# A list scheduler's table of durations and its random term, changed together in a transformer-block kernel

## The chip, the cores and the metric

One core of one Trainium2 chip. The metric is the device time of one execution in microseconds (us); lower is better. The kernel before was run three times: 789.57 us (median), 788.88 and 794.04.

## The reference

One transformer block with adaptive layer norm, on 2048 rows of 512 columns, 32 heads of width 16, in bf16:

```python
mod = (silu(c) @ w_mod).reshape(1, 6, 1, 512)            # sa, ca, ga, sb, cb, gb
h = layernorm(x) * (1 + ca) + sa
q, k, v = split(h @ wqkv)                                # 32 heads, Dh = 16
p = softmax(q @ k.T * Dh ** -0.5)                        # 2048 x 2048 for each head
x = x + ga * ((p @ v).reshape(2048, 512) @ wo)
h = layernorm(x) * (1 + cb) + sb
out = x + gb * (gelu(h @ w1 + b1) @ w2 + b2)             # hidden width 1376
```

The bulk of the work is the exponentials of 32 x 2048 x 2048 scores.

## The kernel before, in words

**Tiling.** Queries go in 4 blocks of 512, keys in 16 tiles of 128. A *run* is four heads over one query block (in the last block: eight heads over half of it); there are 32 runs. For each run and key tile the four heads' scores are made by four matmuls that use 32 rows of the array each. One such piece, 128 keys x 512 queries of one head, is a *unit*: 32 x 16 x 4 = 2048 units in all.

**Two ways to an exponential.** A unit takes one of two ways.

- *ScalarE's way* (`qk_a`, L834): two or three units at a time are put into a PSUM tile `st` (one of three banks, one of two), and one ACTIVATE of 128x1536 or 128x1024 (L872) writes the exponentials to `pt`. One pass of matmuls with V follows for each key tile (`pv_op`, L934, matmuls at L961, into the accumulator `od`).
- *VectorE's way* (`qk_d`, L885, and `shifts`, L923): each unit of a key tile goes to a PSUM tile `ax`; an operation on VectorE (L913) turns it into the bit pattern of a coarse exponential, `ph`. Then four operations of 128x2048 (L928) make shifted copies `sh`; all five patterns are multiplied with copies of V that are scaled to fit (`VX`), so that their errors cancel. A key tile thus costs eight operations on VectorE and five passes of matmuls with V in place of one.

Only key tiles 2, 6, 10 and 14 of a run (in the first run only 14) may go VectorE's way. `next_tile` (L802) decides while the schedule is made: ScalarE first takes a run's other tiles, and then takes a shared tile too if VectorE has not taken it by then.

**Around it.** Layer norm, projections and transposes of the next blocks (`layer_norm`, `make_k`, `make_q`, `make_v`), and for each finished query block the output projection, second layer norm and feed-forward part (`block_tail`, L1154; for the last half block `last_half`, L1224) are strewn between the scores. Each block's Gelu (L1203) makes ScalarE change its function table before and after.

**The order.** The kernel writes out the order of every engine by itself. `Plan` (L103) is a list scheduler that runs while the program is built: each `Op` names its engine, its duration in us, its latency, what it depends on and which buffer it takes. `Plan.step` commits, again and again, the operation with the earliest possible start over all engines. On one engine, `pick` (L146) looks at all that could start within a short slack of the first, and takes the lowest `dyn + spread`: `dyn` (L350) is the priority, for TensorE by the state of the plan (scores for ScalarE 0.0, 2.2 or 6.0; scores for VectorE 1.0; matmuls with V 0.2 or 3.0), and `spread` (L158) is a pseudo-random addition. The planned clock `now` exists only while building; the chip gets four fixed instruction lists and the semaphores. The durations thus do not set how long anything takes. They set which order is written, and how many key tiles go each way.

When the plan finds TensorE idle for too long, it inserts matmuls of zeros (`heat`, L428; `zeros`, L446) that change no result.

The durations in question: `A_US` (L297) is an ACTIVATE of exponentials by its units; `0.6` at L915, L930, L986 and others is an operation of VectorE on 512 float32 columns of PSUM (or 2048 int16 columns of SBUF).

Of the kernel before, what the change touches and what calls it, by code (L numbers as in the profile page):

```python
# [12 lines left out]
ALU = mybir.AluOpType  # L13
# [44 lines left out]
DL = 0.14  # L58
DPL = 0.08
AL = 0.21  # L60
FILL = 1.6
SPREAD = 0.15
SEEDS = (917, 884, 957, 158, 587, 98, 234, 513, 13, 197, 564, 221, 161, 230, 162, 26, 317, 634, 72, 409, 524, 986, 200, 52, 57, 427, 804, 124, 15, 75, 621, 299)
HEAT = 1.3


# [39 lines left out]
class Plan:  # L106
# [49 lines left out]
        return s, o  # L156

    def spread(self, o):  # L158
        x = ((sum(map(ord, o.kind)) if o.eng == "PE" else o.fn.__code__.co_firstlineno if o.fn else 0) * 2654435761 ^ SEEDS[min(int(self.now // 25.0), len(SEEDS) - 1)] * 2246822519) & 0xFFFFFFFF
        x = ((x ^ x >> 15) * 2246822519) & 0xFFFFFFFF  # L160
        return SPREAD * ((x ^ x >> 13) & 1023) / 1024.0

    def ahead(self, can):

# [94 lines left out]
def kernel(  # L259
# [14 lines left out]
    nc = tc.nc  # L274
# [19 lines left out]
    MM = 0.2155  # L294
    SPAN = (3, 2)
    POOL_US, POOL_MIN = 0.68, 0.5
    A_US = {1: 0.475, 2: 0.904, 3: 1.33}  # L297
    AHEAD = 3
    PSUM_F = 8
    FIRST_DKS, D_TIME = (14,), 8.0  # L300
# [335 lines left out]
    def layer_norm(src, deps, mod, mod_dep, hold_z, alloc_h, engines, ps_res, kind, prio,  # L636
                   after=None, nt=TPB):

        ln = op("NIL", None, 0.0, (), lat=0.0, prio=0.0, acq=r_ln)
        st = [op("DVE", lambda o, t=t: stats(ln, t, src(t)), 0.83, (deps[t], ln, after and after[t]), prio=prio)  # L640
              for t in range(nt)]
        rs = [op("POOL", lambda o, i=i: rstd(ln, 2 * i, 2 * i + 2), 1.3,
                 st[2 * i:2 * i + 2] + [o_mh], prio=0.0) for i in range(nt // 2)]
        z = op("NIL", None, 0.0, (rs[0], hold_z), lat=0.0, prio=0.0, acq=r_z)
        za = [op("DVE", lambda o, t=t: apply(ln, z, t, src(t)), 0.33, (z, rs[t // 2]), prio=prio,
                 rel=(ln,), port=True) for t in range(nt)]
        h = op("NIL", None, 0.0, (rs[0],), lat=0.0, prio=0.0, acq=alloc_h)
        done = []
        trs = []
        if isinstance(ps_res, tuple):  # L650
            two = []
            for part in range(2):
                for half in range(2):
                    def tr(o, half=half, part=part):
                        if part:
                            o.tile = two[half].tile
                            two[half].ps = o.tile.bitcast(BF16)
                        ps = o.tile.bitcast(BF16)
                        for j in (2 * half, 2 * half + 1):
                            for t in (2 * part, 2 * part + 1):  # L660
                                nc.tensor.transpose(
                                    out=ps[:, (j % 2) * QB + t * P:(j % 2) * QB + (t + 1) * P],
                                    in_=z.tile[:, t, j * P:(j + 1) * P], identity=ident)
                    one = op("PE", tr, 4 * 0.0705, za[0:2 + 2 * part] + [o_id] + two[half:half + part],
                             lat=PEL, mode=("full", 0), kind=kind,
                             acq=None if part else ps_res[half], rel=(z,))
                    two.append(one)
            trs += two[2:4]
            for half in range(2):
                one, done_tr = two[half], two[2 + half]  # L670
                for j in (2 * half, 2 * half + 1):
                    e = engines[j]
                    done.append(op(e, lambda o, j=j, e=e, one=one: modulate(
                        e, h.tile[:, j, :], one.ps[:, (j % 2) * QB:(j % 2 + 1) * QB], mod, j),
                        0.5 if e == "DVE" else 0.72, (done_tr, mod_dep, h), prio=0.2, rel=(one,)))
        else:
            for j in range(NC):
                def tr(o, j=j):
                    o.ps = o.tile.bitcast(BF16)[:, 0:nt * P]
                    for t in range(nt):  # L680
                        nc.tensor.transpose(out=o.ps[:, t * P:(t + 1) * P],
                                            in_=z.tile[:, t, j * P:(j + 1) * P], identity=ident)
                one = op("PE", tr, nt * 0.0705, za, lat=PEL, mode=("full", 0), kind=kind,
                         acq=r_ax, rel=(z,))
                trs.append(one)
                e = engines[j]
                done.append(op(e, lambda o, j=j, one=one, e=e: modulate(
                    e, h.tile[:, j, 0:nt * P], one.ps, mod, j), 0.13 + nt * 0.1, (one, mod_dep, h), prio=0.1,
                    rel=(one,)))
        return h, done, za, trs  # L690
# [16 lines left out]

    def make_k(b, cc, kind, acq, eng, after=None):
        mm = proj(b, o_w[1], cc, kind, acq, after)
        o_k[(cc, b)] = op(eng, lambda o: copy(eng, kT[cc][b], mm.tile[:, 0:QB]), 0.6 if eng == 'DVE' else 0.5, (mm,), prio=0.3,  # L710
                          rel=(mm,))

    o_qz = [op("POOL", lambda o, n=n, p=p: nc.gpsimd.memset(QM[n][:, p, :], 0.0), 0.5, prio=0.5 + n)
# [2 lines left out]
    def make_q(b, cc, kind, acq):  # L716
        qm = op("NIL", None, 0.0, (), lat=0.0, prio=0.0, acq=r_qm)
        mm = proj(b, o_w[0], cc, kind, acq, after=qm)
        if (b, cc) == (0, 0):
            evs = [op("DVE", lambda o, p=p: nc.vector.tensor_scalar(  # L720
                out=qm.tile[:, p, :], in0=mm.tile[:, 0:QB], scalar1=qmask[:, p:p + 1], scalar2=None,
                op0=ALU.mult), 0.6, (mm, qm, o_mask), prio=0.1 if p == 0 else 0.45, rel=(mm,)) for p in range(2)]
        else:
            qs = op("DVE", lambda o: nc.vector.tensor_scalar(
                out=o.tile, in0=mm.tile[:, 0:QB], scalar1=QSC, scalar2=None, op0=ALU.mult), 0.6, (mm, qm),
                prio=0.3, acq=r_qs, rel=(mm,))

            evs = []
            for p in range(2):
                rows = [dma(lambda o, at=slice(i, i + 16), p=p: nc.sync.dma_start(  # L730
                    out=qm.tile[at, p, :], in_=qs.tile[at, :]), [qs] + o_qz, kb=16, n=1.4, prio=0.4 + p, rel=(qs,))
                    for i in range(16 * p, P, 32)]
                evs.append(op("NIL", None, 0.0, rows, lat=0.0, prio=0.0))
        o_q[(cc, b)] = (qm, evs)
        qm.uses += 1
        q_left[(cc, b)] = 8 * NT

    def make_v(b, cc, kind, acq, eng, after=None):
# [9 lines left out]
        def ev(o):  # L748
            dst = VEB[b][:, :, 8 * cc * VW:8 * (cc + 1) * VW].rearrange(
                "p t (h w) -> p t h w", w=VW)  # L750
            copy(eng, dst[:, :, :, 0:16], mm.tile[:, 0:QB].rearrange("p (t h d) -> p t h d", t=TPB, h=8))
        got = [op(eng, ev, 0.6, [mm] + o_v0[b], prio=0.3, rel=(mm,))]
        for t in DKS:
            if t // TPB == b:
                def scale(o, t=t):
# [129 lines left out]
    def qk_d():  # L885
# [24 lines left out]
        def ex(e):  # L910
# [1 line left out]
            units[0] += 1  # L912
            nc.vector.tensor_scalar(out=ph.tile[:, o.row * QB:(o.row + 1) * QB], in0=o.tile, scalar1=PH_B,  # L913
                                    scalar2=0.0, op0=ALU.add, op1=ALU.max)
        d_e.append(op("DVE", ex, 0.6, (o,), lat=DL, prio=0.5, rel=(o,)))  # L915
        d_e[-1].run = r
        if last:
            shifts(r, kt, ph, list(d_e))
# [4 lines left out]
    def shifts(r, kt, first, es):  # L923
        def parts(o):
            return lambda: [o.tile[:, h * QB:(h + 1) * QB].bitcast(BF16) for h in range(4)]
        pv_op(r, kt, 0, es, parts(first), (first,))
        for j in range(1, NPH):
            sh = op("DVE", lambda o, j=j: nc.vector.tensor_scalar(  # L928
                out=o.tile, in0=first.tile, scalar1=PH_SH[j], scalar2=None, op0=ALU.add),
                0.6, es, lat=DL, prio=2.0, acq=r_sh, rel=(first,), port=True)  # L930
            sh.run = r
            pv_op(r, kt, j, (sh,), parts(sh), (sh,))

# [49 lines left out]

    def normalise(r):
        last, od = o_last[r], o_od[r]
        OD = op("DVE", lambda o: nc.vector.tensor_copy(out=o.tile, in_=od.tile), 0.6, (last,),  # L986
                prio=0.0, acq=r_OD, rel=(od,))
        st = {}

# [164 lines left out]
    def block_tail(b, nt=TPB):  # L1154
# [8 lines left out]
        for t in range(nt):  # L1163
# [1 line left out]
                      [x for u in ots for x in u.two] + [prev], kind, r_ax, ots, 2)  # L1165
            prev = a
            res_done.append(op("DVE", lambda o, t=t, a=a: nc.vector.tensor_tensor(
                out=x2.tile[:, t, :], in0=a.tile, in1=xr.tile[:, t, :], op=ALU.add), 0.6,
                (a, xr), prio=0.1, rel=(a,)))
        h, hd, za, trs = layer_norm(lambda t: x2.tile[:, t, :], res_done, modB, o_late["mB"],  # L1170
                                    None, r_blk, ("DVE",) * 4, r_ax, kind, 0.3, None, nt)
# [10 lines left out]
        for f in range(NF):  # L1182
# [6 lines left out]
            if direct:  # L1189
# [3 lines left out]
                continue  # L1193
            ev.append(op("DVE", lambda o, f=f, mm=mm: nc.vector.tensor_scalar(  # L1194
                out=g.tile[:, f, 0:N], in0=mm.tile[:, 0:N], scalar1=b1c[:, f:f + 1], scalar2=None,
                op0=ALU.add), 0.13 + nt * 0.134, (mm, o_late["b1"]), prio=0.3 if part else 0.1, rel=(mm,)))
        if part:
            ge = [op("ACT", lambda o, lo=lo, hi=hi: nc.scalar.activation(
                out=g.tile[:, lo:hi, 0:N], in_=g.tile[:, lo:hi, 0:N], func=ACT.Gelu_apprx_tanh),
# [10 lines left out]
        for t in range(nt):  # L1210
# [2 lines left out]
                       lambda f: ge[0] if not part else ge[f >= 2] if f < PSUM_F else ev[f])  # L1213
            prev = mm
            a = op("DVE", lambda o, t=t, mm=mm: nc.vector.tensor_tensor(
                out=o.tile, in0=mm.tile, in1=x2.tile[:, t, :], op=ALU.add), 0.6,
                (mm,), prio=3.0 if part else 0.1, acq=r_o, rel=(mm, x2))
            dma(lambda o, t=t, a=a: nc.sync.dma_start(
                out=out[0][b * QB + t * P:b * QB + (t + 1) * P, :], in_=a.tile), (a,), kb=128,
# [234 lines left out]
```

## Time and profile before

| what | us |
|---|---|
| three runs: median, lowest, highest | 789.57, 788.88, 794.04 |
| span of the profiled execution, first to last instruction | 787.2 |
| what lies around the span, if that execution was the median or the lowest run | 2.4 or 1.7 |
| ScalarE busy | 761.3 (97%) |
| TensorE busy (matmuls) | 733.0 (93%) |
| VectorE busy | 719.9 (91%) |
| GpSimd busy | 125.2 (16%) |

The profiled execution has no time of its own in the record beside its span. "Busy" is the time in which at least one instruction of an engine is under way; neighbours on one engine overlap a little, so a group's busy time is less than count x mean duration. Engine names in the profile: PE is TensorE's matmuls and PEld its weight loads, DVE is VectorE, ACT is ScalarE, POOL is GpSimd, SP the engine that issues most DMAs. The columns of a group's row are: line, engine, operation, output<-inputs with shapes and count | busy us, mean ns of one | idle us of the engine just before them, and who ended most of that idle time.

### The profile page before, as it was taken

To read this page: it belongs to the slowest core of one execution; us is meant where nothing else is said; L and a number is where in the kernel's file an instruction comes from. 1 tells how busy PE (TensorE), PEld (TensorE's weight loads), DVE (VectorE), ACT (ScalarE), POOL (GpSimd) and SP (SyncE) were. 2 spreads that over 40 slices of the span, in tenths; PEclk is the share of its full clock that TensorE was granted. 3 is DMA by queue.
4 is the path that set the end of the run, shared out by engine and by line. 5 is a ranking of instruction groups with operands and counts; after the bars stand their busy time and mean duration, and the time that the engine had idled before them with its cause. 6 is when DMAs were issued, how large, how long until landed. Compare 5 with 4: busy or idle time off the path is not lost.

```text
span 787.2 us, 20269 instructions
## 1 busy us (share of the span) xinstructions
PE 733.0 (93%) x8173; PEld 275.0 (35%) x8173; DVE 719.9 (91%) x1253; ACT 761.3 (97%) x689; POOL 125.2 (16%) x279
## 2 busy tenths in 40 slices
PE   8889998999999888988999999998999999999998
PEld 3433333233333322223322323222234344444454
DVE  6878797998999999999999998999999999999874
ACT  4999999999999999999999999999999999999994
POOL 6522501013122430100000200001000100001000
PEclk9999999999999999999999999999999999999999
DMA  7043010000002110000100010000110101000110
GB/s 214 30 134 91 18 50 19 22 23 19 9 20 68 27 42 24 18 23 7 42 21 20 25 32 24 12 20 23 32 50 19 32 19 45 18 18 10 32 50 28
DMA packets 39072, 28.21 MB, mean 36 GB/s; under 512 B 17957, under 2 KB 34374, under 8 KB 38978
## 3 DMA queue, kind: packets, MB, share of 16 engines
q1 hardware_dynamic: 38970, 26.91, 12.1%
q8 instruction: 64, 1.05, 0.5%
q14 instruction: 30, 0.25, 0.1%
q10 hardware_dynamic: 8, 0.00, 0.0%
HBM read 21.30 MB, written 2.61 MB: 30 GB/s over the span
## 4 chain that ended last, share of the span: by engine, by line
ACT 53%; PE 27%; issue 12%; DVE 8%; DMA 0%; POOLq 0%; POOL 0%; SPq 0%; DVEq 0%; ACTq 0%
ACT pt L872 50%; PE od L961 9%; PE st L823 8%; DVE sh L928 3%; DVE ph L913 3%; PE ax L823 2%; PE ax L1184 2%; PE ax L1124 2%; ACT g L1203 1%; PE ax L1118 1%; PE ax L702 1%; PE ax L432 1%; PE t L1124 1%; ACT L872 0%; DMA qm<-qs 0%
## 5 line engine op out<-in xcount | busy, mean ns | idle before, releaser
L872 ACT ACTIVATE pt<-st 128x1536 bf16<-128x1536 f32 x635 | 719.5, 1385 | 2.8 <-PE st L823 2.7
L913 DVE TENSOR_SCALAR ph<-ax 128x512 int16<-128x512 f32 x460 | 301.5, 683 | 21.9 <-PE ax L823 20.0
L928 DVE TENSOR_SCALAR sh<-ph 128x2048 int16<-128x2048 int16 x460 | 301.0, 694 | 1.9 <-PE od L961 1.0
L823 PE MATMUL st<-qm,kT 32*128 32x512 bf16 x1588 | 248.3, 382 | 33.3 <-ACT pt L872 26.9
L823 PEld LDWEIGHTS <-kT 32*128 32x128 bf16 x2048 | 86.8, 91 | 248.8 <-issue 237.5
L823 PE MATMUL ax<-qm,kT 32*128 32x512 bf16 x460 | 159.0, 378 | 5.7 <-DVE ph L913 2.5
L961 PE MATMUL od<-sh,VX 128*32 128x512 bf16 (+1 forms) x2320 | 158.7, 340 | 4.2 <-DVE sh L928 3.2
L961 PE MATMUL od<-pt,VEB 128*32 128x512 bf16 (+1 forms) x1980 | 144.8, 340 | 0.1
L961 PEld LDWEIGHTS <-VEB 128*32 128x32 bf16 x2560 | 62.2, 96 | 73.4 <-issue 59.4
L961 PEld LDWEIGHTS <-VX 128*32 128x32 bf16 x2320 | 55.2, 95 | 79.2 <-issue 69.4
L1013 POOL TENSOR_TENSOR OT<-OD,RB 128x256 bf16<-128x256 f32 x38 | 27.4, 730 | 313.3 <-DVE sh L928 188.7
L961 PE MATMUL od<-ph,VEB 128*32 128x512 bf16 (+1 forms) x580 | 45.4, 338 | 1.3 <-DVE OD L986 1.0
L1013 POOL TENSOR_TENSOR OS<-OD,RB 128x256 bf16<-128x256 f32 x24 | 17.6, 744 | 167.1 <-DVE sh L928 139.4
L1184 PE MATMUL ax<-blk,W 128*128 128x512 bf16 (+1 forms) x164 | 42.2, 361 | 0.5 <-DVE ph L913 0.4
L702 PE MATMUL ax<-blk,w 128*128 128x512 bf16 x124 | 36.8, 382 | 2.0 <-DVE blk L627 0.9
L757 POOL TENSOR_SCALAR VX<-VEB 128x128 bf16<-128x128 bf16 x64 | 24.2, 378 | 53.2 <-DVE VEB L634 49.4
L1194 DVE TENSOR_SCALAR g<-ax,b1c 128x512 bf16<-128x512 f32 (+1 forms) x41 | 28.2, 693 | 4.4 <-PE ax L1184 4.2
L1124 PE MATMUL ax<-w,g 128*128 128x512 bf16 x112 | 30.2, 381 | 0.5 <-DVE ph L913 0.4
L1124 PEld LDWEIGHTS <-g 128*128 128x128 bf16 x176 | 14.6, 97 | 24.5 <-issue 13.0
L608 DVE BATCH_NORM_STATS2 ln_s<-xb 128x6 f32<-128x512 bf16 x32 | 21.7, 677 | 1.4 <-DMA xb<-in_A_x_dram 1.3
L986 DVE COPY OD<-od 128x512 f32<-128x512 f32 x31 | 21.2, 683 | 0.8 <-PE od L961 0.5
L1184 PEld LDWEIGHTS <-W 128*128 128x128 bf16 x176 | 14.1, 97 | 21.3 <-issue 15.3
(110 smaller groups left out, 367.0 us busy)
## 6 DMA issues: line engine op xcount, KB each, us to landing
RB<-rn SPq DMA_DIRECT2D x124, 64.0 KB
xb<-in_A_x_dram SPq DMA_DIRECT2D x8, 512.0 KB
out_dram<-o SPq DMA_DIRECT2D x16, 128.0 KB
qm<-qs SPq DMA_DIRECT2D x120, 16.0 KB
W<-in_B_w_dram SPq DMA_DIRECT2D x1, 1376.0 KB
w<-in_A_wqkv_dram SPq DMA_DIRECT2D x3, 384.0 KB
blk<-in_w_mod_dram SPq DMA_DIRECT2D x2, 512.0 KB
xb<-in_w_mod_dram SPq DMA_DIRECT2D x2, 512.0 KB
```

Of the source, the lines that this page charges most:

```text
L608: nc.vector.bn_stats(out=st6, in_=src)
L702: return chain([(lambda ps, j=j: nc.tensor.matmul(out=ps[:, 0:QB], lhsT=w.tile[:, j, cc * P:(cc + 1) * P], rhs=o_h[b].tile[:, j, :], start ...
L757: nc.gpsimd.tensor_scalar(out=v_cols(VX[(t, ph)])[:, 8 * cc:8 * cc + 8, 0:16], in0=v_cols(v_tile(t, 0))[:, 8 * cc:8 * cc + 8, 0:16], scala ...
L823: nc.tensor.matmul(out=o.tile[:, k * QB:(k + 1) * QB], lhsT=kT[cc][kb][rows, ko * P:(ko + 1) * P], rhs=qm.tile[rows, par, :] if hb is None ...
L872: nc.scalar.activation(out=e.tile[:, 0:len(got) * QB], in_=o.tile[:, 0:len(got) * QB], func=ACT.Exp, scale=ESC)
L913: nc.vector.tensor_scalar(out=ph.tile[:, o.row * QB:(o.row + 1) * QB], in0=o.tile, scalar1=PH_B, scalar2=0.0, op0=ALU.add, op1=ALU.max)
L928: sh = op("DVE", lambda o, j=j: nc.vector.tensor_scalar(out=o.tile, in0=first.tile, scalar1=PH_SH[j], scalar2=None, op0=ALU.add), 0.6, es, ...
L961: nc.tensor.matmul(out=o_od[r].tile[32 * i:32 * i + 32, n * HB:n * HB + w], lhsT=v_tile(kt, ph)[:, c0:c0 + 32], rhs=got[i][:, at:at + w], ...
L1013: two = beside(lambda c: nc.gpsimd.tensor_tensor(out=OT.tile[:, c], in0=OD.tile[:, c], in1=o5.tile[:, c], op=ALU.mult), (OT,), (OD, o5))
L1124: nc.tensor.matmul(out=ps, lhsT=g[:, f, col:col + P], rhs=rhs, start=(f == 0), stop=(f == NF - 1))
L1184: mm = chain([(lambda ps, f=f, j=j: nc.tensor.matmul(out=ps[:, 0:N], lhsT=W1[:, j, f * P:(f + 1) * P], rhs=h.tile[:, j, 0:N], start=(j == ...
L1194: ev.append(op("DVE", lambda o, f=f, mm=mm: nc.vector.tensor_scalar(out=g.tile[:, f, 0:N], in0=mm.tile[:, 0:N], scalar1=b1c[:, f:f + 1], s ...
```

## The change

Two things are changed, both in the scheduler's input. No operation of the kernel gets another form.

- Planned durations: 0.6 becomes 0.655 for VectorE's operations on 512 columns of PSUM (0.7 for the two masked copies of the first Q) and on 2048 columns of int16; the layer norm's `apply` goes from 0.33 to 0.41 (in `layer_norm` alone); the bias addition ahead of Gelu from 0.13 + 0.134 to 0.1 + 0.153 for each 128 columns; the exponentials' from 0.475, 0.904 and 1.33 to 0.49, 0.92 and 1.346 for one, two and three units.
- The random term: it was 0 to 0.15, one draw for each *kind* of operation and each 25 us of planned time. It becomes one draw for each *operation*, with one seed for each 12.5 us, times 0.3 and the remainder of the seed by 4: a range up to 0, 0.3, 0.6 or 0.9. Of the 66 seeds 17 have remainder 0 (no draw), 14 remainder 1, 8 remainder 2 and 27 remainder 3.

```diff
-SPREAD = 0.15
-SEEDS = (917, 884, 957, 158, 587, 98, 234, ...)
+SPREAD = 0.3
+SEEDS = (0, 0, 679, 650, 815, 471, 439, 947, 118, ...)
...
     def spread(self, o):
-        x = ((sum(map(ord, o.kind)) if o.eng == "PE" else o.fn.__code__.co_firstlineno if o.fn else 0) * 2654435761 ^ SEEDS[min(int(self.now // 25.0), len(SEEDS) - 1)] * 2246822519) & 0xFFFFFFFF
+        seed = SEEDS[min(int(self.now // 12.5), len(SEEDS) - 1)]
+        x = (o.seq * 2654435761 ^ seed * 2246822519) & 0xFFFFFFFF
         x = ((x ^ x >> 15) * 2246822519) & 0xFFFFFFFF
-        return SPREAD * ((x ^ x >> 13) & 1023) / 1024.0
+        return SPREAD * (seed % 4) * ((x ^ x >> 13) & 1023) / 1024.0
...
-    A_US = {1: 0.475, 2: 0.904, 3: 1.33}
+    A_US = {1: 0.49, 2: 0.92, 3: 1.346}
...
-        za = [op("DVE", lambda o, t=t: apply(ln, z, t, src(t)), 0.33, ...
+        za = [op("DVE", lambda o, t=t: apply(ln, z, t, src(t)), 0.41, ...
...
-        d_e.append(op("DVE", ex, 0.6, (o,), lat=DL, prio=0.5, rel=(o,)))
+        d_e.append(op("DVE", ex, 0.655, (o,), lat=DL, prio=0.5, rel=(o,)))
...
-                0.6, es, lat=DL, prio=2.0, acq=r_sh, rel=(first,), port=True)
+                0.655, es, lat=DL, prio=2.0, acq=r_sh, rel=(first,), port=True)
...
-                op0=ALU.add), 0.13 + nt * 0.134, (mm, o_late["b1"]), ...
+                op0=ALU.add), 0.1 + nt * 0.153, (mm, o_late["b1"]), ...
```

The same 0.6 to 0.655 is made in `make_k`, `make_q`, `make_v`, `normalise` and twice in `block_tail`. After the change every line from L159 on stands one lower (L872 becomes L873).

## The prediction

> **What bounds the kernel now.** I read the page first (its busy times, then its groups), then the busy time by stage, the waits, and last the timelines of ScalarE and VectorE. The page:
>
> ```profile
> PE 733.0 (93%) x8173; PEld 275.0 (35%) x8173; DVE 719.9 (91%) x1253; ACT 761.3 (97%) x689; POOL 125.2 (16%) x279
> ...
> L872 ACT ACTIVATE pt<-st 128x1536 bf16<-128x1536 f32 x635 | 719.5, 1385 | 2.8 <-PE st L823 2.7
> L913 DVE TENSOR_SCALAR ph<-ax 128x512 int16<-128x512 f32 x460 | 301.5, 683 | 21.9 <-PE ax L823 20.0
> L928 DVE TENSOR_SCALAR sh<-ph 128x2048 int16<-128x2048 int16 x460 | 301.0, 694 | 1.9 <-PE od L961 1.0
> ```
>
> Three engines are above 90%, so the shares decide nothing. The last column does: ahead of its 635 exponentials ScalarE sat idle 2.8 us in all, while VectorE waited 21.9 us for scores. By stage (PE, PEld, DVE, ACT, POOL busy, with counts):
>
> ```profile
> 80.00:200.00 120.00, 112.88 (x1174) 40.41 (x1171) 104.59 (x179) 120.00 (x107) 24.50 (x48) 1.00 0.10 25
> 200.00:320.00 120.00, 110.39 (x1165) 37.88 (x1163) 119.11 (x198) 120.00 (x107) 29.20 (x50) 1.00 0.11 32
> 320.00:440.00 120.00, 112.36 (x1079) 35.96 (x1076) 117.44 (x206) 119.94 (x104) 11.16 (x17) 1.00 0.08 21
> 440.00:560.00 120.00, 113.26 (x1059) 35.18 (x1062) 115.50 (x193) 119.94 (x103) 8.68 (x13) 1.00 0.09 24
> 560.00:680.00 120.00, 113.55 (x1699) 47.64 (x1691) 114.91 (x198) 118.18 (x105) 9.11 (x14) 1.00 0.12 33
> ```
>
> ScalarE is full in each; it did 107 exponentials in the stage where VectorE had 15 us to spare and 107 in the one where VectorE was full. The waits say the same from TensorE's side: it waits for ScalarE to free score banks, not the reverse.
>
> ```profile
> PE st L823 <- ACT pt L872: 26.9, 87, 0.8
> ...
> ACT pt L872 <- PE st L823: 2.7, 4, 0.9
> ```
>
> The ends of the body, from ScalarE's timeline (start, us):
>
> ```profile
> 15.16 6.88 ACT L872 ACTIVATE pt<-st 128x1536 bf16<-128x1536 f32 x6 [0.49 <-PE st L823]
> ...
> 712.71 51.27 ACT L872 ACTIVATE pt<-st 128x1536 bf16<-128x1536 f32 x45
> 764.00 1.28 ACT L1198 ACT_TABLE_LOAD   x1
> ```
>
> So the span is 15.2 us of start, a body of 748.8 on ScalarE, and a tail of 23.2. From instruction to instruction in that trace, one exponential ends 1.343 us after the one before it if it has three units, 0.917 if two (medians; quarter points within 0.002). 318 of the one and 317 of the other make 717.8. Three Gelu visits (4.90 plus two table loads of 1.28 each) make 22.4, other evictions in the body about 5; some 3 to 4 us are left as losses. That is all a better order could win there.
>
> **The change, part by part.** *How many tiles go each way.* The changed program's instruction lists, counted, have 320 exponentials of 1536 and 320 of 1024 (before 318 and 317), and 448 operations at each of VectorE's two lines (before 460). So 2048 - 448 = 1600 units go ScalarE's way, not 1588: three key tiles change sides. The planner believes VectorE slower, so it is later in taking shared tiles and ScalarE takes them.
>
> ScalarE gets 2 x 1.343 + 3 x 0.917 = **+5.4 us**. This lies on the path: before and after it ScalarE is full. Check by the group's row: 719.5 / 1588 = 0.453 a unit, x 12 = 5.4.
>
> VectorE loses 24 operations. Is one of them 0.655 us, as the change says? 301.5 / 460 = 0.655 is busy time of a group, with the overlap of each with its neighbour from the other line counted in. Back to back they start closer:
>
> ```profile
> 61.88 3.09 DVE L928 TENSOR_SCALAR sh<-ph 128x2048 int16<-128x2048 int16 x5
> ...
> 71.41 1.88 DVE L913 TENSOR_SCALAR ph<-ax 128x512 int16<-128x512 f32 x3
> ```
>
> (3.09 - 0.69) / 4 = 0.60 and (1.88 - 0.68) / 2 = 0.60: the old value is the pace, the new one a duration. VectorE is given 24 x 0.60 = 14.4 us less, and that buys nothing where ScalarE binds. I take it as 0. Its cover is ScalarE's body; if that weren't full, it could be worth up to 14.4 (rival below). The Trainium skill ("VectorE: DVE Perf Modes", section "The DRAIN you can't avoid") says that the next operation doesn't start until the pipe has emptied, though a next one that isn't held may start earlier. By the first half a shift would cost its 0.694 and 24 of them 16.7 us; the rows above show starts 0.60 apart, so the trace goes with the second half.
>
> TensorE: three tiles take one pass with V in place of five, 12 passes fewer; 52 matmuls of zeros are added at the accumulator (136 for 84). The zeros' row has 8.2 us for 84, so at most 5.1 us; 12 passes of four at 0.06 us a matmul give 2.9 back. Net at most +2 against 40 us of TensorE's idle time between 80 and 764: 0, and +2 if that cover failed.
>
> *The planned exponentials.* 0.92 + 1.346 = 2.266 a pair, against 2.260 measured and 2.234 planned before. The plan may now put 16 ns more work ahead of a refill. Most refills have hundreds of ns to spare; if a tenth of 635 have none, that is 64 x 0.016 = 1.0. I keep it in the next term.
>
> *The order, drawn anew.* TensorE's list differs nearly everywhere, and with it VectorE's, GpSimd's and SP's (the late weights' loads and the reciprocal's small DMAs move by several places). None waits visibly in ScalarE's way now; what such waits cost shows in the losses by stage: 0.00, 0.00, 0.06, 0.06, 1.82 us. Bounds: all losses go, -3.0; every stage loses as much as the worst, 6 x 1.82 = 10.9 in place of 3.6, +7.3. Nothing in the lists says which; VectorE will be early where the plan waits for it, which speaks for few new waits, wider draws against. I take 0, the row it has now.
>
> *Start.* The order up to the first exponential is the same on ScalarE. On TensorE two zero matmuls (0.215 each) come in among the transposes, and four transposes (0.056 each) move behind the modulation's matmuls: bounds -0.1 and +0.6, I take +0.3. One x block's load stands one weight load later, which ScalarE's three short waits there (0.2 to 0.5 us) could feel; that is inside the same bound.
>
> *Tail.* The same operations, three of them better placed: the last three feed-forward groups of the half block (12 matmuls) are done ahead of the last score, and the second half's transposed copies on ScalarE stand behind 7 of the first half's 11 Gelus, not all. From the copy on, TensorE has 52 small matmuls at 0.058 and 21 at 0.216 to do, 7.6 us, where it had 44 and 25, 8.0. I take -0.4; bounds -1.5 (the whole first difference, 12 at 0.1, too) and +0.5 (the product at L1264 stands behind 7 matmuls of the feed-forward part in place of 5).
>
> Sum: 787.2 + 5.4 + 0.3 - 0.4 + 0 = **792.5 us of span**. Around the span lay 2.4 if the profiled execution was the median run (1.7 if the lowest). I take 2.4: **794.9 us**, 0.7% above the median of 789.57.
>
> **The rivals.** *Late refills (slower by more than 1%).* The new order leaves score banks empty more often; ScalarE's losses rise. For: a 1536 exponential often starts just 0.1 us after its last score matmul, so margins are thin. Against: TensorE's list, summed by 100 units with the trace's mean start-to-start times, holds 35 to 44 us in every stage without a Gelu from unit 100 on, where ScalarE takes 45.2. It decides from 2.6 us of further losses (797.5); at the bound of 7.3 it is 802.2.
>
> *Losses vanish (about 790 to 792).* The fuller plan removes the 3 us that ScalarE lost: 791.9; with the best start and tail (-0.4 and -1.1 more) 790.4.
>
> *VectorE was the bound (faster).* If its full stages (119.11 of 120) set the pace, 24 operations fewer take 14.4 us off, and the three tiles hide beside: 789.57 - 14.4 = 775.2. It decides only if ScalarE waits for work, which in those stages it did for 0.00 us. The skill's rule on the drain would raise it to 16.7 and 772.9; that rule's second half takes it away again.
>
> *The change does nothing.* Excluded for the counts; for the time it needs the 5.4 to be hidden, that is, exponentials put into idle time. ScalarE's idle time lies in start and tail, where no scores exist.
>
> **How the numbers follow.** Forecast (5.4 stays, losses within about 2.5 of now; 792.5 to 797.4): 0.72. Late refills 0.19. Losses vanish 0.06. VectorE the bound 0.03. A measurement here tells about 1% from no change, 781.7 to 797.5. Faster 0.03, within 1% 0.72 + 0.06 = 0.78, slower 0.19. The range reaches down to all losses gone, 790.5, and up to 800.5, a little over half of the late refills' reach; some 0.12 is left out.
>
> **What will show it.** In the changed profile: ScalarE's exponentials x640, busy 719.5 + 5.4 = about 725; its idle time ahead of them still a few us; first one near 15.4 and last one's end near 769.5; VectorE's two lines x448 with about 294 us each, and its share below 91%; operations of VectorE still 0.60 apart. I am wrong if ScalarE's stages between 80 and 760 lose several us each, or if exponentials end closer than 1.343 and 0.917 apart.

## The result, and the profile after

The changed kernel takes 798.96 us (median of 11 runs, 796.45 to 799.48); the kernel before, run beside it and before, 791.15 (11 runs, 788.51 to 797.26). The ratio is 1.0098, 95% interval 1.0077 to 1.0119: slower, by a little under 1%. The profiled execution took 799.31 us, 1.8 more than its span of 797.5.

The page of the changed kernel (its lines stand one lower than before):

```profile
PE 736.2 (92%) x8146; PEld 271.0 (34%) x8146; DVE 715.4 (90%) x1229; ACT 767.4 (96%) x694; POOL 121.6 (15%) x279
...
PEclk9999998999999999999999999999999999999999
...
L873 ACT ACTIVATE pt<-st 128x1536 bf16<-128x1536 f32 (+1 forms) x640 | 725.5, 1367 | 6.6 <-PE ax L824 4.4
L914 DVE TENSOR_SCALAR ph<-ax 128x512 int16<-128x512 f32 x448 | 298.2, 685 | 34.6 <-PE ax L824 29.4
L929 DVE TENSOR_SCALAR sh<-ph 128x2048 int16<-128x2048 int16 x448 | 295.0, 693 | 3.0 <-PE od L962 2.2
```

The exponentials' row grew by 6.0 us of busy time, and the idle time in front of them from 2.8 to 6.6. VectorE has less to do and waits more. And one digit of TensorE's clock row is an 8 where there were only 9s. By stage (PE, PEld, DVE, ACT, POOL busy, then the granted clock, DMA share, GB/s):

```profile
80.00:200.00 120.00, 111.54 (x1167) 40.22 (x1167) 106.22 (x179) 118.56 (x106) 26.18 (x56) 0.97 0.08 22
200.00:320.00 120.00, 107.20 (x1094) 34.42 (x1094) 111.23 (x183) 117.51 (x105) 26.23 (x42) 0.97 0.12 34
320.00:440.00 120.00, 112.84 (x1062) 35.49 (x1054) 112.02 (x192) 119.94 (x104) 10.48 (x17) 1.00 0.09 24
440.00:560.00 120.00, 114.82 (x1096) 35.43 (x1088) 113.05 (x187) 119.94 (x104) 8.68 (x13) 1.00 0.08 22
560.00:680.00 120.00, 110.77 (x1548) 45.00 (x1545) 111.32 (x188) 118.71 (x106) 9.22 (x14) 0.99 0.11 30
```

In the first two stages, where ScalarE was full before, it now loses 1.4 and 2.5 us, and the granted clock there is 0.97 where it was 1.00. The last stage, at 0.99, is no worse for ScalarE than before (118.71 us busy, 118.18 before). VectorE is full nowhere. ScalarE's timeline gives the ends of the body and the places of its two longest waits:

```profile
15.13 5.97 ACT L873 ACTIVATE pt<-st 128x1536 bf16<-128x1536 f32 x5 [0.49 <-PE st L824]
...
261.43 43.05 ACT L873 ACTIVATE pt<-st 128x1024 bf16<-128x1024 f32 x38 [1.22 <-PE ax L824]
305.75 4.62 ACT L873 ACTIVATE pt<-st 128x1024 bf16<-128x1024 f32 x4 [1.27 <-PE ax L824]
...
774.24 1.28 ACT L1199 ACT_TABLE_LOAD   x1
```

Around three of the four places at which the clock fell, each in two stretches, one ahead of the fall and one at half clock:

```profile
117.80:121.20 3.40, 2.38 (x33) 1.15 (x32) 3.32 (x6) 3.40 (x4) 2.76 (x5) 1.00 0.00 0
121.20:128.00 6.80, 6.80 (x61) 1.79 (x63) 4.80 (x14) 5.64 (x6) 2.66 (x4) 0.50 0.04 6
...
298.70:302.10 3.40, 2.90 (x23) 0.73 (x24) 3.33 (x6) 3.40 (x4) 1.41 (x2) 1.00 0.09 19
302.10:305.50 3.40, 3.23 (x27) 0.84 (x26) 2.22 (x4) 2.38 (x3) 0.00 (x0) 0.50 0.52 172
...
629.80:633.20 3.40, 2.26 (x35) 0.85 (x33) 3.13 (x9) 3.40 (x4) 0.67 (x2) 1.00 0.00 0
633.20:636.60 3.40, 3.40 (x38) 1.20 (x41) 1.89 (x5) 2.13 (x2) 0.25 (x1) 0.50 0.06 10
```

Ahead of each fall TensorE is busy for 2.3 to 2.9 of 3.4 us; in the stretch at half clock (6.8 us at the first place, 3.4 at the others) ScalarE, always full until then, loses 1.0 to 1.3 us. TensorE's timeline at the second of these shows how:

```profile
300.93 0.81 PE L824 MATMUL ax<-qm,kT 32*128 32x512 bf16 x2
302.26 0.61 PE L824 MATMUL st<-qm,kT 32*128 32x512 bf16 x3 [0.52 <-ACT pt L873]
302.81 0.62 PE L962 MATMUL od<-pt,VEB 128*32 128x512 bf16 x4
303.21 0.64 PE L449 MATMUL od<-warm 128*32 128x512 bf16 x4
303.64 0.64 PE L962 MATMUL od<-ph,VEB 128*32 128x512 bf16 x4
304.06 0.64 PE L449 MATMUL od<-warm 128*32 128x512 bf16 x4
304.49 0.64 PE L962 MATMUL od<-ph,VEB 128*32 128x512 bf16 x4
305.06 0.58 PE L824 MATMUL st<-qm,kT 32*128 32x512 bf16 x2
```

A pass of four with V now takes 0.64 where it takes 0.40 at full clock, and starts 0.43 after the one before it. The plan's own zeros (L449), meant to keep the clock up, come just behind the fall and stand ahead of the refill: five passes at the slow pace lie between the two score refills, and the exponential behind them starts 1.27 us late.

**A budget for every run.** ScalarE's body can be split without remainder. *Exponentials* is their number by their pace, 1.343 and 0.917 us from end to end, which held in every kernel. *Losses* is what their ends lie further apart than that. *Other* is ScalarE's remaining work in the body with its waits. Start and tail are what lies around the body. All in us, from the one profiled execution of each kernel; medians and ratios from all runs. One execution is not the median: those of e5 and e9 were the fastest of their runs, those of e2 and e10 the slowest, and the four runs of e9 have spans from 795.7 to 802.2.

| kernel | start | exponentials | other | losses | tail | span | clock | median, ratio to before (95%) |
|---|---|---|---|---|---|---|---|---|
| before | 15.2 | 717.8 | 27.5 | 3.5 | 23.2 | 787.2 | 1.000 | 791.15 |
| changed | 15.1 | 723.2 | 28.1 | 7.7 | 23.3 | 797.5 | 0.989 | 798.96, 1.0098 (1.0077 to 1.0119) |
| e1 changed, four stretches filled | 15.5 | 723.2 | 28.1 | 5.2 | 23.4 | 795.4 | 0.996 | 798.59, 1.010 (1.0076 to 1.0125) |
| e2 durations alone | 15.2 | 728.6 | 28.1 | 9.4 | 26.3 | 807.7 | 0.985 | 806.48, 1.0207 (1.0177 to 1.0237) |
| e3 draws alone | 14.3 | 719.6 | 27.5 | 16.8 | 24.4 | 802.7 | 0.983 | 803.86, 1.0171 (1.0141 to 1.0201) |
| e4 no zeros, another order | 15.1 | 717.8 | 27.5 | 10.6 | 25.9 | 796.9 | 0.981 | 799.52, 1.012 (1.0092 to 1.0147) |
| e5 changed, idle waits filled | 15.2 | 723.2 | 28.1 | 1.7 | 23.9 | 792.2 | 1.000 | 795.23, 1.0072 (1.0045 to 1.010) |
| e6 before, idle waits filled | 14.6 | 717.8 | 27.5 | 4.3 | 23.2 | 787.4 | 0.998 | 790.54, 1.0011 (0.9989 to 1.0032) |
| e7 before, no zeros | 15.8 | 717.8 | 27.5 | 7.8 | 23.2 | 792.2 | 0.989 | 794.61, 1.005 (1.0032 to 1.0069) |
| e8 changed, VectorE's old durations | 15.2 | 717.8 | 27.6 | 14.9 | 24.3 | 799.8 | 0.994 | 801.6, 1.014 (1.0113 to 1.0166) |
| e9 no draws, old durations | 15.8 | 719.6 | 27.5 | 8.7 | 24.0 | 795.7 | 0.993 | 801.87, 1.0145 (1.0109 to 1.0181) |
| e10 no draws, new durations | 15.8 | 728.6 | 28.1 | 12.2 | 23.6 | 808.4 | 0.983 | 807.18, 1.0215 (1.0179 to 1.025) |
| e11 before, steadied | 15.0 | 717.8 | 27.5 | 3.1 | 23.2 | 786.8 | 1.000 | 789.21, 0.9976 (0.9953 to 0.9999) |
| e12 changed, steadied | 15.3 | 723.2 | 28.4 | 4.7 | 23.3 | 795.0 | 0.996 | 796.8, 1.0062 (1.0034 to 1.0089) |

The changed kernel's span is 10.3 above the profiled one of before: 5.4 in exponentials, 4.2 in losses, 0.6 in a wait of ScalarE's for a K projection at 24 us, 0.1 elsewhere. The execution of before that was profiled had its clock at 1.000 throughout; of the 67 runs of it beside e1 to e12 only 7 had.

### The profile page after: what moved, and what is told of

The parts are those of the page before. It is cut to its first block, busy times and chain, and to the rows that moved or that the text cites. A ratio compares the mean times of both kernels' runs of the same rounds, so it can differ in the third digit from the quotient of the medians.

```text
span 797.5 us, 20077 instructions
## 1 busy us (share of the span) xinstructions
PE 736.2 (92%) x8146; PEld 271.0 (34%) x8146; DVE 715.4 (90%) x1229; ACT 767.4 (96%) x694; POOL 121.6 (15%) x279
## 4 chain that ended last, share of the span: by engine, by line
ACT 67%; PE 18%; issue 13%; DVE 1%; DMA 1%; SPq 0%; ACTq 0%; DVEq 0%
ACT pt L873 63%; PE od L962 5%; PE st L824 5%; ACT g L1204 2%; PE ax L1185 1%; PE ax L703 1%; PE ax L1125 1%; DMA blk<-in_w_mod_dram 1%; PE ax L824 1%; PE t L1297 1%; PE t L1125 1%; ACT blk L625 1%; ACT L873 0%; PE od L449 0%; DVE ph L914 0%
## 5 line engine op out<-in xcount | busy, mean ns | idle before, releaser
L873 ACT ACTIVATE pt<-st 128x1536 bf16<-128x1536 f32 (+1 forms) x640 | 725.5, 1367 | 6.6 <-PE ax L824 4.4
L914 DVE TENSOR_SCALAR ph<-ax 128x512 int16<-128x512 f32 x448 | 298.2, 685 | 34.6 <-PE ax L824 29.4
L929 DVE TENSOR_SCALAR sh<-ph 128x2048 int16<-128x2048 int16 x448 | 295.0, 693 | 3.0 <-PE od L962 2.2
L824 PE MATMUL st<-qm,kT 32*128 32x512 bf16 x1600 | 252.3, 385 | 46.4 <-ACT pt L873 40.2
L824 PEld LDWEIGHTS <-kT 32*128 32x128 bf16 x2048 | 88.5, 91 | 270.3 <-issue 259.5
L962 PE MATMUL od<-sh,VX 128*32 128x512 bf16 (+1 forms) x2240 | 161.7, 342 | 2.2 <-DVE sh L929 1.4
L962 PE MATMUL od<-pt,VEB 128*32 128x512 bf16 (+1 forms) x2000 | 152.9, 345 | 1.8 <-ACT pt L873 1.1
L1014 POOL TENSOR_TENSOR OT<-OD,RB 128x256 bf16<-128x256 f32 x38 | 28.1, 750 | 324.4 <-DVE sh L929 237.5
L962 PEld LDWEIGHTS <-VX 128*32 128x32 bf16 x2240 | 52.8, 95 | 67.4 <-issue 58.6
L758 POOL TENSOR_SCALAR VX<-VEB 128x128 bf16<-128x128 bf16 x64 | 21.1, 329 | 44.7 <-DVE VEB L635 41.4
L742 PE MATMUL ax<-w,blk 128*128 128x128 bf16 x256 | 20.9, 220 | 0.3
```

The lines of the kernel that those rows point to most:

```text
L824: nc.tensor.matmul(out=o.tile[:, k * QB:(k + 1) * QB], lhsT=kT[cc][kb][rows, ko * P:(ko + 1) * P], rhs=qm.tile[rows, par, :] if hb is None ...
L873: nc.scalar.activation(out=e.tile[:, 0:len(got) * QB], in_=o.tile[:, 0:len(got) * QB], func=ACT.Exp, scale=ESC)
L929: sh = op("DVE", lambda o, j=j: nc.vector.tensor_scalar(out=o.tile, in0=first.tile, scalar1=PH_SH[j], scalar2=None, op0=ALU.add), 0.655, e ...
L962: nc.tensor.matmul(out=o_od[r].tile[32 * i:32 * i + 32, n * HB:n * HB + w], lhsT=v_tile(kt, ph)[:, c0:c0 + 32], rhs=got[i][:, at:at + w], ...
L1014: two = beside(lambda c: nc.gpsimd.tensor_tensor(out=OT.tile[:, c], in0=OD.tile[:, c], in1=o5.tile[:, c], op=ALU.mult), (OT,), (OD, o5))
```

## The experiments

**Theory after the result.** Two things add up: twelve units moved to ScalarE at 0.452 us each, and an order in which the granted clock falls to half for 3.4 us or a multiple at some places, where ScalarE then starves. That thin use of TensorE's array makes the clock fall there is the guess behind it. **Rival:** the new order refills the score banks late by itself, and the clock is a side effect.

**e1: fill the four stretches.** Zero passes add 0 to the accumulator, so no result changes; the order is otherwise that of the changed kernel.

```diff
+            n_pv[0] += 1
+            if left[r] > 0:
+                for _ in range(FILLED.get(n_pv[0] - 1, 0)):
+                    zeros(r)
```

> The changed kernel, its order untouched, with 19 passes of zero matmuls added behind the matmuls with V in the four stretches (115 to 121, 252 to 258, 297 to 302 and 627 to 633 us) before its granted clock fell to half. Theory (thin work on TensorE lets the clock fall, and the slow clock starves ScalarE): the granted clock stays 1.00, the losses of 1.8, 1.3, 1.4 and 1.4 us in the stages at 120, 240, 280 and 600 go, the span falls from 797.5 to about 792.5, the time from 799.0 to about 794. Rival (the new order refills the score banks late, the clock falls because TensorE then waits): the clock may stay up, but the losses stay, span 796 to 799.

Measured: 798.59, no better. At the four places the clock did stay up, and their losses went (that at 120 to 0.3, that at 632 to 0.5), but it fell at two others, 246 and 317 us. The clock of the six runs was 0.991 to 0.998, so how much is lost differs from run to run. Its time is not the 794 of the theory, and neither side is settled by it, for the clock didn't stay up; of the losses of 5.2, 2.3 sat at or right behind the two falls.

**e2 and e3: each half of the change alone.**

```
 e2: the changed kernel with SPREAD, SEEDS and spread() of the kernel before
 e3: the kernel before with SPREAD, SEEDS and spread() of the changed one
```

> The new durations with the old random term. Its lists hold 322 and 323 exponentials (1612 units, 24 more than before) and 436 operations at each of VectorE's two lines. Theory (a unit moved to ScalarE costs 0.452 us, on the path): 10.8 us more than before from the units alone, about 800 if the clock holds, 802 to 806 if it falls a few times. Rival (truer durations make a better order, the draws spoil it): less than 5 us more than before, under 795.

> The old durations with the new random term. Its lists hold 318 and 319 exponentials (1592 units, 4 more) and 456 operations at each of VectorE's two lines. Theory (the units set the body; the clock falls where an order leaves TensorE thin): 1.8 us more than before if the clock holds, each stretch of 3.4 us at half clock about 1.2 us more. Rival (the wide draws themselves cost the time): as slow as the changed kernel, 796 to 800, with the clock at 1.00.

Measured: 806.5 and 803.9, both slower than the two together. e2 was a little over its range: exponentials +10.8, as forecast, losses 9.4, and a tail longer by 3.1. e3 is the miss: with four units more than before it lost 16.8 us, in some 30 places, 10.3 of it at or just behind a half clock and 6.5 elsewhere. Neither expectation held for it. Eight stretches of 3.4 us at half clock would make 1.8 + 8 x 1.2 = 11.4 us by the theory, and the span grew by 15.5; the rival wanted a clock of 1.00, which was 0.983, and a time of 796 to 800.

**e4 and e7: the kernel before without its plan's zeros.**

```diff
     def zeros(r):
-        for i in range(4):
-            nc.tensor.matmul(out=o_od[r].tile[32 * i:32 * i + 32, :], lhsT=warm[:, 0:32],
-                             rhs=warm[:, 0:1].to_broadcast([P, QB]), start=False, stop=False,
-                             tile_position=(0, 32 * i))
+        pass
```

> The kernel before, its order untouched, with the 21 passes of zero matmuls left out that its plan put in to keep TensorE busy. Theory (the clock falls after a stretch of about 3.4 us with too little work): the clock falls at some of those 21 places, 3 to 12 of them, each stretch costs ScalarE about 1.2 us, time 794 to 805. Rival (the zeros do nothing): the clock stays 1.00 and the time that of before, within 1 us.

> The kernel before, its order untouched, without the 21 passes of zero matmuls that its plan put in. This replaces the run before it of the same intent, whose order had changed too (the old random term hashes line numbers, and the edit had moved lines). Theory: the clock falls at several places, below 0.99, each stretch of 3.4 us at half clock adds about 1.2 us to ScalarE's losses of 3.5, time 794 to 803. Rival: clock and time as before, 789 to 792.

e4 measured 799.52, but the three lines that it lost moved the line numbers that the old random term hashes, and the whole order with them; it tells nothing of the zeros alone. e7 keeps the lines, and its order is that of before but for the 21 passes. It takes 794.61, ratio 1.005; in all ten runs the clock is 0.985 to 0.991. In the windows of its trace, its longest fall, with TensorE busy for 9.64 of 10 us and the granted clock at 0.50:

```profile
125.00:135.00 10.00, 9.64 (x73) 2.01 (x73) 4.75 (x9) 8.29 (x8) 1.10 (x2) 0.50 0.09 28
```

That stretch cost 2.2 us of losses, the two others 1.2 each. So work that computes nothing is worth 0.5% here, and without it the losses go from 3.5 to 7.8, by what sits behind the half-clock stretches. The order was the same and TensorE had less to do: here the clock is the cause and no side effect.

**e5 and e6: fill the idle waits of both kernels.** `after` adds zero passes behind the operations of TensorE that a list names.

```diff
-            o.fn(o)
+            o.fn(o); self.after(o)
```

> The changed kernel, its order untouched, with 63 passes of zero matmuls put in at the 59 places where its trace shows TensorE idle for 0.25 us or more between 45 us and the last score. Theory (the half clock makes ScalarE's losses, and the twelve units the rest): granted clock near 1.00, losses of 7.7 us fall to 2 or 3, span 791.5 to 793, time 793.5 to 795, still about 5.4 us behind the kernel before at full clock. Rival (the new order refills the score banks late by itself): losses stay at 5 or more, time 797 to 800.

> The kernel before, its order untouched, with 62 passes of zero matmuls put in at the 55 places where its trace shows TensorE idle for 0.25 us or more. Theory: its runs, whose granted clock was 0.989 to 0.999 beside the profiled one's 1.000, all come near 1.00, and the median falls from 791 to 788.5 to 789.5. Rival (the spread of its runs has another cause): median 791 and the same spread.

e5 is the changed order, with its profiled execution at full clock throughout (span and mean clock of the core first, then the exponentials' row of its page):

```profile
core 0: 792.2 us, clock 1.000
```

```profile
L873 ACT ACTIVATE pt<-st 128x1536 bf16<-128x1536 f32 (+1 forms) x640 | 724.7, 1381 | 1.3 <-PE st L824 1.0
```

The losses are 1.7 us, fewer than in the kernel before, and as many as the changed kernel has away from its four falls (7.7 - 5.9 = 1.8). The rival falls: at full clock the new order refills in time. Three of six runs had a clock of 1.000 and spans of 792.2, 792.6 and 793.2; the others, at 0.991 to 0.997, took 793.5 to 797.4, so the median came to 795.23, just over the range. e6 missed: nothing gained, clock 0.991 to 1.000. Filling the idle waits held the clock in half of e5's runs; in the order of before it changed nothing.

**e8: VectorE's durations back.**

```diff
-        d_e.append(op("DVE", ex, 0.655, (o,), lat=DL, prio=0.5, rel=(o,)))
+        d_e.append(op("DVE", ex, 0.6, (o,), lat=DL, prio=0.5, rel=(o,)))
 ... and the other planned durations of VectorE alike
```

> The changed kernel with VectorE's planned durations put back to the old ones, 0.60 and the like; the new random term and the new exponentials' durations stay. Its lists hold 318 and 317 exponentials (1588 units, as before) and 460 operations at each of VectorE's two lines, and 35 passes of zeros in the body. Theory (VectorE's durations took the twelve units, the draws make the order thin): the 5.4 us of units go, exponentials 717.8 us as before, losses 5 to 12, span 789 to 795, time 791 to 797. Rival (the durations cost nothing by themselves, the draws all): time 797 or more, as the changed kernel.

The units went back to 1588 and the 5.4 us with them, as forecast, but the losses came to 14.9, above the range, of which 6.6 around one fall of 10.2 us at 592 and the rest in many small waits. The time is 801.6, in the range of the rival and not of the theory. Some 8 us of these losses, like the 6.5 of e3, are at no half clock: in other orders ScalarE does wait for scores at full clock too. What the seeds do for one set of durations they don't do for another.

**e9 and e10: no draws.**

```diff
 e9:  -SPREAD = 0.15  +SPREAD = 0.0      e10:  -SPREAD = 0.3  +SPREAD = 0.0
```

> The kernel before with its random term set to 0: the old durations alone make the order. Its lists hold 318 and 319 exponentials (1592 units). Theory (seeds are what keeps an order's losses low; each fits one set of durations): exponentials 1.8 us more than before, losses 8 to 17 in place of 3.5, time 796 to 806. Rival (the old durations make a good order by themselves): losses about 4, time 791 to 794.

> The changed kernel with its random term set to 0: the new durations alone. Its lists hold 322 and 323 exponentials (1612 units), 20 more than the same with the old durations. Theory (a unit costs 0.452 us, and the new durations give no better order): 9.0 us of exponentials more than the old durations without draws, losses about the same as there (8 to 17), time 804 to 815. Rival (truer durations make a smoother order): losses 4 or less, so that it comes within 4 us of the old durations without draws.

Without draws the new durations cost 20 units: 728.6 - 719.6 = 9.0 us of exponentials. Losses are 8.7 and 12.2 and the times 801.87 and 807.18, all in the ranges that were expected. Whether the new durations make a smoother order is open: the medians are 5.3 apart, less than the 9.0 of the units alone, while the profiled executions, e9's fastest run and e10's slowest, are 12.7 apart. The rival (losses of 4 or less, within 4 us) failed. With their draws the old order falls to 3.5 of losses and 1588 units, the new one to 7.7 and 1600: each set of seeds suits its durations. The new seeds save 12 units (1612 to 1600) and the old ones 4 (1592 to 1588), so that of the 20 units between them 12 are left.

**e11 and e12: zeros where the array is thinly used.** Each matmul of 512 columns was counted as 0.216 us (the pace of full ones in the tail) from its start on, times the share of the array's rows or columns that it uses. Zeros were put in wherever this weighed use was below 0.40 over any 3.4 us, by the means of e5.

The traces say which 3.4 us count. In each of them all falls lie whole multiples of 3.413 us apart, as if on a grid, whose place in the span differs from execution to execution. Over those windows of the grid that lie at full clock, from 16 us to 25 us before the end, the changed kernel's four lowest values, 0.29, 0.31, 0.33 and 0.36, are those of the four windows just ahead of its falls; the next is 0.38. The kernel before, whose profiled execution had no fall in its span (its grid is taken from one 1.2 us behind the end), has none below 0.41. TensorE's busy share tells less: it is 0.67 to 0.86 ahead of the four falls, and the changed kernel's lowest, 0.62 ahead of 418 us, had no fall behind it.

> The kernel before, its order untouched, with 33 passes of zeros put in where the work of its matmuls, weighed by the share of the array that each uses, is below 0.40 of any 3.4 us of its trace. Theory (what lets the clock fall is thin use of the array, not idle time): the clock stays at 0.998 or more in all runs and the median falls to 788.5 to 789.5. Rival (as with passes put in at idle waits): no change in clock or time, median within 1 us of before, some runs at 0.99.

> The changed kernel, its order untouched, with 34 passes of zeros put in by the same rule as in the steadied kernel before (where the weighed use of the array is below 0.40 in any 3.4 us of its trace). Theory (the change costs twelve units, 5.4 us, and the half clock the rest): clock 0.998 or more in nearly all runs, losses 2 to 3, span 792, median 793.5 to 794.5, so 4.5 to 5.5 behind the steadied kernel before's 789.2. Rival (the new order costs something of its own besides): 796 or more at full clock.

e11 did what e6 did not: the clock of its 12 runs is 0.998 to 1.000, their times 788.48 to 790.42 where the 17 beside them of the kernel before ran from 787.19 to 796.81. With 33 passes, half of e6's 62, it is the fastest kernel here, 0.9976 of before, barely clear of no difference; what it takes away is most of the falls. Two of its runs, at 0.998, still lost as much clock as one fall costs (e6's profiled execution, at 0.998, has one of 3.41 us); of the 17 of before 16 are at 0.998 or less. The exponentials' row of its page:

```profile
L872 ACT ACTIVATE pt<-st 128x1536 bf16<-128x1536 f32 x635 | 719.7, 1376 | 2.3 <-PE st L823 2.1
```

e12 missed: 796.8, clock 0.991 to 0.998. Its profiled execution fell once at 18 us, ahead of the first pass that was put in (55.8 us), and once again at 301. Its places were chosen from one trace with half-clock stretches in it, and the grid's place differs from execution to execution; that either of these is why it missed is argued, not shown. Nothing here holds the changed order at full clock in every run.

## Why the prediction was right and where it was wrong

*What binds.* Right. ScalarE stayed the bound; VectorE lost 24 operations, 4.5 us of busy time by the page, and only waited more (34.6 for 21.9).

*Twelve units, +5.4.* Right, to the tenth: 717.8 to 723.2, at an unchanged pace. The kernels with other counts (1592, 1600, 1612 units) keep the same pace.

*VectorE's pace, 0.60 and not 0.655.* Right: back to back its two lines start 0.60 to 0.61 us apart in both kernels (medians 0.601 and 0.602 before, 0.607 and 0.602 after). The planner was given a duration that includes the overlap with the next operation, and so gave tiles away that VectorE had time for (e8: 1588 units with 0.60). VectorE's two rows came to 298.2 and 295.0 us, where the prediction had about 294 each. The first half of what the Trainium skill says ("VectorE: DVE Perf Modes", section "The DRAIN you can't avoid") doesn't bind here, the second half (an operation that isn't held starts earlier) does.

*The planned exponentials, up to 1.0.* No run changes these durations alone, so the term stays open. Its ground, that most refills have hundreds of ns to spare, does not hold for the exponentials of three units, and the prediction's own first rival said so: in the trace of before half of them start within 0.17 us of the end of their last score matmul, a quarter within 0.11 (of those of two units half within 0.39).

*Start +0.3, tail -0.4.* Both wrong by their size and without weight: 0.0 and +0.1. A wait for a K projection at 24 us, 0.6, was not in the sum.

*The order drawn anew, taken as 0.* This is the step that failed. It measured +4.2 in the profiled execution, inside its bounds (-3.0 to +7.3), but I took the row that the kernel before had, on the ground that VectorE would be early where the plan waits for it. What the runs showed in its place is the granted clock, which stood in neither bound nor rival: the new order lets it fall to half at four places, and e5, the same order at full clock, loses 1.7 us. Around the four falls lie 5.9 us of losses, against a total of 3.5 before. I had read a clock row of 9s and priced TensorE's thinner work, 12 passes fewer and 13 of zeros more, at nothing, with idle time as its cover. That cover was the wrong one: not TensorE's idle time in 684 us counts, but what it does in single stretches of 3.4. The zeros are the plan's own mark of where it found TensorE too idle; 34 passes of them for 21 could have been a warning. The rival of late refills described what ScalarE saw; its argument against, TensorE's sums by 100 units, was true and useless, since 45 us hide a thin 3.4.

*The base.* The forecast span, 792.5, is close to that of the changed order at full clock (792.2 in e5). That is partly luck: e5's losses are 1.8 us below those of before, and the K projection's wait and a longer tail take 0.6 and 0.7 back. Three things lay between it and the time. Around the span lie 1.8 us, not 2.4. The profiled execution of before was one at full clock; 16 runs of before at 0.998 or more have a mean span of 786.7, 19 at 0.985 to 0.991 one of 791.2. And the changed order is nearly always at the lower clock: its runs and those of e1, e5 and e12 have 793.5 at 0.998 or more (7 runs) and 797.1 at 0.985 to 0.991 (14). So at like clock the change costs about 6 to 7 us, though none of the seven is the changed kernel without added zeros; the rest of the 7.8 between the medians is that it is more often at half clock. That left 798.96 inside the range of 790.5 to 800.5 but 4.1 above the forecast, and clear of no change, where I had given most of the chance to a move too small to tell.

## What to carry to other kernels

When a planner is fed from a trace, give it start-to-start times: a duration counts the overlap with the next operation, and a planner that balances two engines by it moves work to the wrong one; here 9% on VectorE's operations cost ScalarE, which was full, 12 units at 0.452 us (e8), and 20 or 24 together with the other durations where the seeds were not made for them (e10, e2). The truer time alone made no faster kernel, though: e8 got its 12 units back and lost more by its order. In a kernel whose TensorE is busy but thinly used, read the granted clock at the scale at which it falls (3.4 us) and in several runs, for a single profiled execution at 1.000 says little, and ask of each reordering whether a stretch of small or partial matmuls comes of it. Draws and durations that were tuned together are one change: each half alone was slower here than both.

## What the runs showed of the hardware

TensorE's granted clock fell to 0.50 while TensorE was busy for 2.26 to 2.90 of the 3.40 us ahead, with no gap over 0.8 us at those places. Falls last 3.41 us or two or three times that, and in each trace they begin whole multiples of 3.413 us apart. The Trainium skill ("TensorE: Matmul & The Clock Gate", section "Part 1: The HAM clock gate (the "warmup" mystery)") puts the fall after an idle window of about 3.4 us that runs freely; the lengths and the grid agree. If that is read as a wholly idle window, it does not agree.

What told the places apart was use weighed by the share of the array, over the windows of the grid. In the 14 traces, 35 windows between 16 us and 25 us from the end were followed by a fall; their weighed use is 0.14 to 0.39 and TensorE's busy share in them 0.41 to 0.89. Of the other windows at full clock, none of the 2952 at 0.40 or more was followed by one; below 0.30 all nine were; between, 26 of 67. A sharp limit does not come out of these runs (some matmuls are missing from the traces), and the count was made from the traces afterwards, so it shows where the clock fell and not why.

A single stretch of 3.4 us at half clock cost ScalarE's stream 0.7 to 1.6 us, 1.2 in the median of 23. Over the 67 runs of the kernel before that stood beside e1 to e12, the span grows by some 0.45 us for each 0.001 of mean clock lost.
